# Moving one broadcast, some sums and one root in the middle of a two-layer mixer kernel

## The chip, the cores and the metric

The kernel runs on one NeuronCore of one Trainium2 chip. The metric is device time in microseconds (us). Before the change the median of three runs is 1218.71 us (1217.93 to 1219.3). Names of engines: PE is TensorE, DVE is VectorE, ACT is ScalarE, POOL is GpSimd, SP is the engine whose queue issues the transfers.

## The reference

Two layers of the same two blocks act on `x` (2048 tokens by 1024 channels, bfloat16). The weights of both layers are the same.

```python
def _A_ref(x, wqkv, wo):            # 32 heads of 32; window of 8 keys, 2 tokens apart
    ...
    logits = jnp.where(mask[None, None, :, :], logits, -1e9)
    attn = _softmax(logits, axis=-1)
    o = jnp.einsum("bhsw,bhswd->bhsd", attn, vg)
    ...
def _B_ref(x, w1, b1, w2, b2):      # a mixer over the tokens, 2048 -> 3584 -> 2048
    h = _layernorm(x, axis=-1)
    u = jnp.einsum("bsd,sf->bdf", h, w1) + b1
    u = _gelu(u)
    y = jnp.einsum("bdf,fs->bds", u, w2) + b2
    ...
x = x + _A_ref(_layernorm(x, axis=-1), A_wqkv, A_wo)
x = x + _B_ref(_layernorm(x, axis=-1), B_w1, B_b1, B_w2, B_b2)
# and both once more
```

## The kernel before, in words

The tokens are dealt to two residue classes (`c` = 0, 1), for the window steps by two; each class has 8 tiles (`i` = 0 to 7) of 128 tokens. `hT` holds the normalised input, transposed, 16 such tiles side by side. A layer goes through these stages:

- V = h · Wv. In the first layer `start_up` makes it plainly; in the second `Sevens.run` (L446 to 486) makes it with seven block products in place of eight.
- attention, in 32 visits (the loop over `vis`): scores, exponentials, mask, values, and the q and k of the next head group (L500). `qk_chunk` copies parts of q into `qB`, some of them with DMAs on SP (L513).
- the output projection (L616), then `gemm1` (L871), the first product of the mixer.
- the second product of the mixer: `gemm2f` in the first layer, `gemm2s` in the second. `gemm2f` normalises its output as well, transposes it into `hT` for the second layer, and makes V's sums ready.

**The products by sevens** take a 2x2 blocking of both factors. Sums and differences of blocks (`S`, `T`, `U`, on DVE, POOL and ACT) are multiplied, and results run through the banks of PSUM: PE makes a product, ACT copies the bank to a second one, and PE adds the next product to that copy. So a copy on ACT stands between two products of PE. The factors are float16, scaled by a power of two that keeps the sums in range. The power comes from a bound of the weights: a maximum by partition, stored to DRAM, read back by a broadcast to all partitions (`share_wv`, L400; `share_w2`, L756), reduced by DVE, and cut to its power of two (`powers`, L732). For V the bound of Wv is known in `start_up` (`top_wv` writes `mv2`, L345); `power_wv` (L405) makes `csv` and `civ`, which `Sevens.scale` (L412) and V's last steps use.

**`gemm2f`** (L1177 on) goes through 8 groups `i` of 256 output columns. Groups 0 and 1 are made plainly: four outputs each, of 28 matmuls (`tokens`, L1316 to 1321). In this time ACT takes bounds of the w2 columns still to come (`bounds`, L797): SP fetches a piece into a free place (`refill`, eight places in `hT` at first), ACT runs over it (L792). `share(4)` and `share(6)` broadcast the bounds for groups 4, 5 and 6, 7. Groups 2 to 7 go by sevens (`product`, L1223 to 1227, 14 matmuls each); while PE works at group `i`, ACT and DVE make the scaled blocks and sums for `i + 1` (`scaled`, `mix`). Each output tile is closed by `corner_add` or `quarter`, then `aggregate` (store to `xb`, mean and variance), `root` (two small ACT instructions) and `normalise` (DVE, then a transposing DMA into `hT`). Group 7 has no successor; there the four tiles of Wv are scaled (`sv[0].scale`) and V's sums made: `t_sum(n, j)` differences of Wv's blocks, `s_sum(i, n)` sums of blocks of token tile `i`, four for each of 8 tiles. The first two token tiles get their sums inside `gemm2f`, the others in `Sevens.run` (`ahead`), a pair ahead.

**What sets the order.** Each engine works strictly in the order of its queue. `chain_(engine, f)` (L232) pins an instruction behind the last one so placed on that engine, `in_order` does it for PE, so the order of the source is the order of the queues. Tiles come from pools with a fixed number of buffers, in rotation; a new tile waits for the last readers of the buffer it takes. The pools that matter are `w` (9 buffers: weights, `T`, `U2`), `q` (2 buffers: `qB`, `qa`, `Sw`), `go` (14 buffers: `g`, `oT`, `qs`, `Sv`), `pc` (2 buffers: `pc`, `bc`, `bcw`, `bcv`) and `x2` (6 buffers).

The start of `gemm2f`, in the order of its queues:

```python
        load_w(1)
        chain_("SP", share_wv)
...
        corner_add(0, 0, 1)
        power_wv()
        in_order(tokens, 0, 1)
        bounds(A, 5)
        del room[:5]
        share(4)
        refill(4)
```

Of the kernel before, what the change touches and what calls it, by code (L numbers as in the profile page):

```python
# [13 lines left out]
FP16 = mybir.dt.float16  # L14
# [3 lines left out]
P = 128  # L18
# [10 lines left out]
def kernel(  # L29
# [15 lines left out]
    nc = tc.nc  # L45
# [31 lines left out]
    qp = pool("qp", 2)  # L77
# [154 lines left out]
    def chain_(eng, f, *args, **kw):  # L232
        with tc.issue_after(last[eng].ins) if eng in last else nullcontext():
            last[eng] = f(*args, **kw)
# [161 lines left out]
    def fill_wv(wv):  # L396
        for j in range(KD // 2):
            chain_("SP", lambda: nc.sync.dma_start(out=wv[j][:], in_=wq_v[:, 2 * j:2 * j + 2, 2 * D:3 * D]))

    def share_wv():  # L400
        bcw["v"] = pcp.tile([P, P, 2], FP32, name="bcv", tag="pc")
        nc.sync.dma_start(out=mxvd[:], in_=mv2[:])
        return nc.sync.dma_start(out=bcw["v"][:], in_=mxvd[:].partition_broadcast(P))

    def power_wv():  # L405
        chain_("DVE", powers, 0, 1, bcw.pop("v")[:].rearrange("p q c -> p (q c)"), csv, civ)

    class Sevens:
# [21 lines left out]
            return hT[:, 4 * c:4 * c + 4, cols(r, i)]  # L430

        def s_sum(self, i, n):
            if i not in self.S:
                self.S[i] = gop.tile([P, 4, 4, P], FP16, name="Sv", tag="go")
            q = [self.S[i][:, k] for k in range(4)]
            x, y, op = [(self.a(i, 1, 0), self.a(i, 1, 1), ALU.add), (q[0], self.a(i, 0, 0), ALU.subtract),
                        (self.a(i, 0, 0), self.a(i, 1, 0), ALU.subtract), (self.a(i, 0, 1), q[1], ALU.subtract)][n]
            chain_("DVE", tt, nc.vector, q[n], x, y, op)
# [326 lines left out]
    def power_w2(i0):  # L765
        def ts(out, in0, sc):
            return nc.vector.tensor_scalar(out=out, in0=in0, scalar1=sc, scalar2=None, op0=ALU.mult)
        i1 = i0 + 2
        chain_("DVE", powers, i0, i1, bcw.pop(i0)[:].rearrange("p q i -> p i q"), cs2, ci2)
        k = st("k2", [P, 2])  # L770
        chain_("DVE", ts, inv2[:, i0:i1], ci2[:, i0:i1], gi[:])
        chain_("DVE", ts, ncs2[:, i0:i1], cs2[:, i0:i1], -1.0)
        chain_("DVE", ts, k[:], cs2[:, i0:i1], gs[:])
        b0, b1 = b2_sb[:, i0:i1, 0], b2_sb[:, i0:i1, 1]
        chain_("DVE", tt, nc.vector, bia[:, i0:i1, 0], b0, k[:], ALU.mult)
        chain_("DVE", tt, nc.vector, bia[:, i0:i1, 1], b1, b0, ALU.subtract)
        chain_("DVE", tt, nc.vector, bia[:, i0:i1, 1], bia[:, i0:i1, 1], k[:], ALU.mult)
# [399 lines left out]
    def gemm2f(g, src, dst, seam):  # L1177
# [59 lines left out]
        def load_w(i, ns=range(4)):  # L1237
            w.setdefault(i, [])
            for n in ns:
                f0, f1 = n * 8, min(n * 8 + 8, FT)  # L1240
                w[i].append(wt_("w2", [P, f1 - f0, 256]))
                chain_("SP", nc.sync.dma_start, out=w[i][n][:], in_=w2_v[:, f0:f1, i * 256:(i + 1) * 256])
# [66 lines left out]
        room[:] = [hT[:, m:m + 4, (c * NI + i) * P:(c * NI + i + 2) * P] for i in (6, 4) for c in range(DIL) for m in (0, 4)]  # L1309
        refill(8)  # L1310
        load_w(1)
        chain_("SP", share_wv)
        chain_(A, ln_exp_table)
        grp = [(0, 1), (1, 1), (0, 0), (1, 0)]

# [9 lines left out]
        bounds(A, 4)  # L1325
        corner(0, 0, 1, bk[0][0])
        corner_add(0, 0, 1)
        power_wv()
        in_order(tokens, 0, 1)
        bounds(A, 5)  # L1330
        del room[:5]
# [61 lines left out]
        for i in range(2, NI):  # L1393
            j = i + 1
            more = j < NI
            pa, pd, pb, pc = (t_[:] for t_ in (two("a") + two("m") if i % 2 else two("s") + two("s")))
            A22, S1, S2, S4 = q[i][:, 0], q[i][:, 1], U2[i], U4[i]
            load_x(i)
            in_order(product, pa, stripes(i, 0, 0), B11)
            chain_(A, move, pb, pa, scale=cs2[:, i:i + 1], bias=bia[:, i, 0:1])  # L1400
            if i == 2:
                corner(1, 1, 0, bk[1][3])
                corner_add(1, 1, 0)
            else:
                quarter(i - 1, 1, 0, prev)
            aggregate(i - 1, 1)
            root(i - 1, 1)
            mix(S4, S4, S2, ALU.subtract)
            normalise(i - 1, 1)
            in_order(product, pd, weights(S1), T1)  # L1410
            if more:
                units_a(j)
            Z = x2("z", [P, 512], FP32)
            if i == 2:
                chain_(A, move, Z[:], pd)
                scaled(j, q[j][:, 0], 1, 1)
            else:
                if more:
                    scaled(j, q[j][:, 0], 1, 1)
                else:  # L1420
                    sv[0].scale(0)
                chain_(A, move, Z[:], pd)
                if more:
                    scaled(j, q[j][:, 1], 0, 1)
                else:
                    sv[0].scale(2)
            in_order(product, pb, weights(S2), [T2k(k) for k in range(K)], False)
            mix(S1, A22, S2, ALU.subtract)
            S3 = S1
            if i == 2:  # L1430
                t4(*range(8, K))
                power_w2(6)
            chain_(A, move, pc, pb, bias=bia[:, i, 1:2])
            if i == 2:
                scaled(j, q[j][:, 1], 0, 1)
            if more:
                units_b(j)
                scaled(j, U2[j], 0, 0, range(2))
                mix(q[j][:, 1], q[j][:, 1], q[j][:, 0], ALU.add)
            in_order(product, pa, stripes(i, 1, 0), B21, False)  # L1440
            if i + 2 < NI:
                load_w(i + 2)
            else:
                seam(i + 2 - NI)
            corner(i, 0, 0, pa)
            corner_add(i, 0, 0)
            if more:
                scaled(j, U2[j], 0, 0, range(2, 4))
            else:
                sv[0].scale(1)  # L1450
                sv[0].scale(3)
                sv[0].t_sum(3, 0)
                sv[0].t_sum(1, 0)
            in_order(product, pc, weights(S3), NT3, False)
            Y = x2("y", [P, 512], FP32)
            chain_(V, tt, nc.vector, Y[:], Z[:], pc, ALU.add)
            quarter(i, 1, 1, Y[:])
            if more:
                mix(U2[j], q[j][:, 1], U2[j], ALU.subtract)
            else:  # L1460
                sv[0].t_sum(3, 1)
                sv[0].t_sum(1, 1)
            in_order(product, pb, weights(S4), B22, False)
            chain_(V, tt, nc.vector, Z[:], Z[:], pb, ALU.add)
            quarter(i, 0, 1, Z[:])
            if more:
                units_c(j)
                scaled(j, U4[j], 1, 0)
            aggregate(i, 0)
            root(i, 0)  # L1470
            normalise(i, 0)
            if not more:
                for n in range(2):
                    for m in range(2):
                        sv[0].s_sum(m, n)
                for m in range(2):
                    sv[0].t_sum(2, m)
            in_order(product, pc, weights(A22), [T4k(k) for k in range(K)], False)
            prev = pc
        i = NI - 1  # L1480
        quarter(i, 1, 0, prev)
        aggregate(i, 1)
        root(i, 1)
        for n in range(2):
            for m in range(2):
                sv[0].s_sum(m, 2 + n)
        for m in range(2):
            sv[0].t_sum(4, m)
        normalise(i, 1)

    sv = [None]
    NU = NG * DIL
# [1 line left out]
    for li in range(2):  # L1494
# [4 lines left out]
        if first:  # L1499
            wv, wts = load_wv(), [None, None]  # L1500
            start_up(v, wv)
            chain_("SP", load_qk, 0, wts)
            res = lambda c, i: xin_v[c, i]
        else:
            def ahead(p, n):
                if p == 2 and n == 0:
                    chain_("DVE", zero_p)
                elif p == 4 and n == 0:
                    chain_("DVE", zero_q)
                elif n and p + 2 < NI:  # L1510
                    for m in range(4):
                        for k in range(2):
                            sv[0].s_sum(p + 2 + k, m)

            sv[0].run(v, ahead)
            res = lambda c, i: rows(xb, c, i)
# [6 lines left out]
            in_order(qk_chunk, 0, wts, part, n)  # L1523
        for vis in range(2 * NU):
            u, b = divmod(vis, 2)
            if b == 0 and u % (2 * DIL) == 1 and u + 3 < NU:
                nxt = [None, None]
                chain_("SP", load_qk, u // (2 * DIL) + 1, nxt)
# [77 lines left out]
        def seam(n):  # L1606
            if n:
                chain_("SP", load_qk, 0, wts)
                return
            wv[:] = load_wv()  # L1610
            fill_wv(wv)
            sv[0] = Sevens(wv)

        gemm2f(g, xa[li], xb, seam)
        qB = new_qB()


# [28 lines left out]
```

## Time and profile before

| | |
|---|---|
| median of three runs | 1218.71 us |
| the profiled execution | 1215.23 us |
| its span, first to last instruction | 1213.5 us |
| mean granted PE clock | 0.996 |
| busy: PE, DVE, ACT, POOL | 1197.1, 779.6, 692.6, 124.8 us |
| plain groups 0 and 1 of `gemm2f` (L1319) | 432.42 to 480.77 us |
| groups 2 to 7 by sevens (L1225) | 480.77 to 618.43 us |
| V by sevens (L442) | 618.43 to 671.89 us |

The profile is of one execution. The rows of a timeline give the start in us from the first instruction, the time, the engine, the line of the kernel and `out<-in` by tile names; in brackets stands how long the engine had been idle, and which event ended this. DMAs are seen where SP issues them (SPq) and by the waits that their landing ends. The granted clock is the share of its full rate that PE was given. Busy time of an engine that nobody waits for costs nothing; what counts is where PE stands still.

### The profile page before, as it was taken

To read this page: it belongs to the slowest core of one execution; us is meant where nothing else is said; L and a number is where in the kernel's file an instruction comes from. 1 tells how busy PE (TensorE), PEld (TensorE's weight loads), DVE (VectorE), ACT (ScalarE), POOL (GpSimd) and SP (SyncE) were. 2 spreads that over 40 slices of the span, in tenths; PEclk is the share of its full clock that TensorE was granted. 3 is DMA by queue.
4 is the path that set the end of the run, shared out by engine and by line. 5 is a ranking of instruction groups with operands and counts; after the bars stand their busy time and mean duration, and the time that the engine had idled before them with its cause. 6 is when DMAs were issued, how large, how long until landed. Compare 5 with 4: busy or idle time off the path is not lost.

```text
span 1213.5 us, 20522 instructions
## 1 busy us (share of the span) xinstructions
PE 1197.1 (99%) x7972; PEld 549.1 (45%) x7972; DVE 779.6 (64%) x1513; ACT 692.6 (57%) x1164; POOL 124.8 (10%) x121
## 2 busy tenths in 40 slices
PE   9999999999999999899989999999999999999998
PEld 4444444444444444344434444444444444444444
DVE  7558887888786634956565588888711312785664
ACT  5657776578777775565645577764543434432342
POOL 0000000280000050000000000002821212100000
PEclk9999999999999999899999999999999999999999
DMA  8822333696766768866520222334946554165521
GB/s 243 148 62 71 84 104 96 216 264 169 216 193 181 222 169 187 189 162 174 166 70 18 62 69 69 112 100 154 304 139 178 176 171 147 62 191 132 155 78 35
DMA packets 248562, 174.12 MB, mean 143 GB/s; under 512 B 48401, under 2 KB 224785, under 8 KB 245137
## 3 DMA queue, kind: packets, MB, share of 16 engines
q1 hardware_dynamic: 248464, 172.82, 51.3%
q8 instruction: 62, 1.02, 0.4%
q14 instruction: 36, 0.29, 0.1%
HBM read 130.30 MB, written 30.43 MB: 132 GB/s over the span
## 4 chain that ended last, share of the span: by engine, by line
PE 89%; DMA 5%; DVE 2%; SPq 1%; ACT 1%; issue 0%; DVEq 0%
PE m L500 18%; PE s L871 11%; PE m L616 9%; PE s L1075 7%; PE m L871 7%; PE a L871 6%; PE s L1225 5%; PE m L1075 4%; PE s L297 3%; PE a L1075 3%; PE s L697 2%; PE a L1225 2%; PE m L1225 2%; PE s L531 2%; PE s L442 2%; DMA mxd<-mx 2%
## 5 line engine op out<-in xcount | busy, mean ns | idle before, releaser
L500 PE MATMUL m<-hT,wqk 128*128 128x512 bf16 x1024 | 231.8, 380 | 0.0
L547 DVE TENSOR_TENSOR Pm<-pc,band 32x640 bf16<-32x640 bf16 x256 | 123.6, 483 | 45.1 <-ACT pc L535 38.3
L500 PEld LDWEIGHTS <-wqk 128*128 128x128 bf16 x1024 | 95.3, 98 | 117.9 <-issue 10.7
L871 PEld LDWEIGHTS <-Sw 128*128 128x128 f16 x832 | 81.4, 98 | 99.2 <-issue 1.2
L616 PE MATMUL m<-wo,oT 128*128 128x512 bf16 x512 | 111.8, 379 | 0.0
L871 PEld LDWEIGHTS <-w 128*128 128x128 f16 (+1 forms) x624 | 61.1, 98 | 73.6
L711 POOL TENSOR_TENSOR T<-h 128x512 f16<-128x512 bf16 x16 | 18.4, 1153 | 621.9 <-DMA xr<-xb 372.9
L616 PEld LDWEIGHTS <-oT 128*128 128x128 bf16 x512 | 49.6, 98 | 60.6 <-issue 1.8
L711 DVE TENSOR_TENSOR py<-pz,m 128x512 f32<-128x512 f32 x14 | 9.6, 687 | 90.4 <-PE m L871 62.1
L535 ACT ACTIVATE pc<-s,shift 128x320 bf16<-128x320 f32 x128 | 60.8, 530 | 11.2 <-PE s L531 11.2
L871 PE MATMUL s<-T,Sw 128*128 128x512 f16 x288 | 66.2, 379 | 0.9 <-ACT s L880 0.9
L507 ACT CAST qs<-m 128x512 bf16<-128x512 f32 x64 | 37.5, 585 | 44.4 <-PE m L500 42.0
L504 ACT CAST kT<-m 128x512 bf16<-128x512 f32 x64 | 37.5, 585 | 41.9 <-PE m L500 38.8
L711 POOL TENSOR_TENSOR Pm<-g 128x512 f16<-128x512 bf16 x24 | 27.7, 1168 | 283.0 <-ACT Pm L792 164.2
L623 DVE TENSOR_TENSOR xn<-m,xr 128x512 bf16<-128x512 f32 x64 | 44.1, 689 | 15.2 <-PE m L616 15.0
L871 PE MATMUL a<-h,w 128*128 128x512 bf16 x224 | 52.9, 379 | 0.0
L871 PE MATMUL m<-T,Sw 128*128 128x512 f16 x224 | 52.9, 379 | 0.0
L656 ACT ACTIVATE h<-xn,bi,rs 128x1024 bf16<-128x1024 bf16 x32 | 39.7, 1240 | 23.1 <-DVE bi L642 23.1
L847 ACT ACTIVATE w<-w,cs 128x2048 f16<-128x2048 bf16 x26 | 51.8, 1997 | 0.0
L1075 PEld LDWEIGHTS <-u 128*128 128x128 f16 x336 | 32.8, 98 | 39.7
L711 DVE TENSOR_TENSOR xs<-tq,xs 128x512 bf16<-128x512 f32 (+1 forms) x30 | 21.2, 710 | 45.1 <-ACT tq L1230 27.9
L511 DVE COPY qB<-qs 32x512 bf16<-32x512 bf16 x136 | 38.2, 281 | 18.5 <-ACT qs L507 15.6
(251 smaller groups left out, 2189.0 us busy)
## 6 DMA issues: line engine op xcount, KB each, us to landing
w<-in_B_w_dram SPq DMA_DIRECT2D x110, 512.0 KB, 6.0
sd<-Sw SPq DMA_DIRECT2D x13, 1024.0 KB, 8.3
Sw<-sd SPq DMA_DIRECT2D x13, 1024.0 KB, 4.9
wqk<-in_A_wqkv_dram SPq DMA_DIRECT2D x16, 512.0 KB, 4.9
xa<-xn SPq DMA_DIRECT2D x32, 256.0 KB, 2.8
xs<-xa SPq DMA_DIRECT2D x32, 256.0 KB, 3.2
Pm<-in_B_w_dram SPq DMA_DIRECT2D x26, 256.0 KB, 6.4
wo<-in_A_wo_dram SPq DMA_DIRECT2D x8, 512.0 KB, 5.4
```

Of the source, the lines that this page charges most:

```text
L500: mm = nc.tensor.matmul(ps[:], lhsT=wts[part][:, kt, (g % 2) * P:(g % 2 + 1) * P], rhs=hT[:, kt, lo:lo + 512], start=(kt == 0), stop=(kt = ...
L511: nc.vector.tensor_copy(out=qB[u % 2][hp, h, ls], in_=qs[hp, :])
L535: nc.scalar.activation(out=pc[:, 2 * n:2 * n + 2].rearrange("p t h k -> p (t h k)"), in_=ss[n][:, 0:2 * HG * GW], func=ACT.Exp, scale=scal ...
L547: mm = nc.vector.tensor_tensor(out=Pm[rp, :, s0:s0 + HB, r * KG:r * KG + GW].rearrange("p h t k -> p t h k"), in0=pc[rp], in1=mk, op=ALU.mult)
L616: mm = nc.tensor.matmul(ps[:], lhsT=oT[g][:, cols(c, i)], rhs=wo[n][g // 4][:, g % 4, :], start=(g == 0), stop=(g == NG - 1))
L623: return nc.vector.tensor_tensor(out=xn[:, xs_], in0=pss_["o", n][:], in1=xr[:, xs_], op=ALU.add)
L656: last["ACT"] = nc.scalar.activation(out=h2[c][i][:], in_=xn[:], func=ACT.Identity, bias=t["bi"][:], scale=t["rs"][:])
L711: return eng.tensor_tensor(out=out, in0=a, in1=b, op=op)
L847: return nc.scalar.activation(out=w[:].bitcast(FP16), in_=w[:], func=ACT.Identity, scale=cs[:, fb + 1:fb + 2])
L871: r = nc.tensor.matmul(out, lhsT=lhs[:, k, :], rhs=rhs[k], start=start and k == 0, stop=stop and k == NI - 1, skip_group_check=True)
L1075: r = nc.tensor.matmul(out, lhsT=lhs[k], rhs=rhs[k][:, cols_], start=start and k == 0, stop=k == K - 1, skip_group_check=True)
L1225: r = nc.tensor.matmul(out, lhsT=lhs[k], rhs=rhs[k], start=start and k == 0, stop=k == K - 1, skip_group_check=True)
```

## The change

1. `share_wv` is split. The store of the bound to DRAM (`keep_wv`) is issued by SP in visit 5 of the first layer's attention. The broadcast back is issued by SP in group 3 of `gemm2f`, after `load_w(5)`, no longer at the start of `gemm2f`.
2. `power_wv` moves on DVE from the start of `gemm2f` to group 5.
3. In group 7 all eight sums of the first two token tiles, and the differences `T3`, `T1`, `T2`, are made earlier on DVE. These sums get one tile of their own in the `q` pool; before they were two tiles of the `go` pool. `scale(1)` and `scale(3)` move on ACT ahead of a bank copy of group 7.
4. The last `root` and `normalise` leave `gemm2f`: they come back as the function `rest`, which `Sevens.run` calls after its first four ACT instructions (two bank copies and two Z).

```diff
+    def keep_wv():
+        return nc.sync.dma_start(out=mxvd[:], in_=mv2[:])
+
     def share_wv():
         bcw["v"] = pcp.tile([P, P, 2], FP32, name="bcv", tag="pc")
-        nc.sync.dma_start(out=mxvd[:], in_=mv2[:])
         return nc.sync.dma_start(out=bcw["v"][:], in_=mxvd[:].partition_broadcast(P))
...
         def s_sum(self, i, n):
+            if i == 0 and n == 0:
+                both = qp.tile([P, 2, 4, 4, P], FP16, name="Sv", tag="q")
+                self.S[0], self.S[1] = both[:, 0], both[:, 1]
...
         load_w(1)
-        chain_("SP", share_wv)
         chain_(A, ln_exp_table)
...
         corner_add(0, 0, 1)
-        power_wv()
         in_order(tokens, 0, 1)
...
                 power_w2(6)
+            if i == 5:
+                power_wv()
+            if not more:
+                sv[0].scale(1)
+                sv[0].scale(3)
+                for n in range(4):
+                    for m in range(2):
+                        sv[0].s_sum(m, n)
             chain_(A, move, pc, pb, bias=bia[:, i, 1:2])
...
                 load_w(i + 2)
+                if i == 3:
+                    chain_("SP", share_wv)
             else:
                 seam(i + 2 - NI)
+            if not more:
+                for m in range(2):
+                    sv[0].t_sum(3, m)
+                    sv[0].t_sum(1, m)
             corner(i, 0, 0, pa)
             corner_add(i, 0, 0)
             if more:
                 scaled(j, U2[j], 0, 0, range(2, 4))
-            else:
-                sv[0].scale(1)
-                sv[0].scale(3)
-                sv[0].t_sum(3, 0)
-                sv[0].t_sum(1, 0)
...
             else:
-                sv[0].t_sum(3, 1)
-                sv[0].t_sum(1, 1)
+                for m in range(2):
+                    sv[0].t_sum(2, m)
...
-            if not more:
-                for n in range(2):
-                    for m in range(2):
-                        sv[0].s_sum(m, n)
-                for m in range(2):
-                    sv[0].t_sum(2, m)
...
         aggregate(i, 1)
-        root(i, 1)
-        for n in range(2):
-            for m in range(2):
-                sv[0].s_sum(m, 2 + n)
         for m in range(2):
             sv[0].t_sum(4, m)
-        normalise(i, 1)
+
+        def rest():
+            root(i, 1)
+            normalise(i, 1)
+
+        return rest
...
             def ahead(p, n):
-                if p == 2 and n == 0:
+                if p == 0 and n == 0:
+                    rest()
+                elif p == 2 and n == 0:
...
+            if first and vis == 5:
+                chain_("SP", keep_wv)
...
-        gemm2f(g, xa[li], xb, seam)
+        rest = gemm2f(g, xa[li], xb, seam)
```

## The prediction

> **What bounds the kernel now.** I read the page first: TensorE (PE) is busy 1197.1 us of a span of 1213.5, and 89% of the chain that ended last is PE. So only time in which PE stands, or runs at a lower clock, can be won. The waits of PE give that time by line.
>
> ```profile
> PE s L1225 <- ACT s L1230: 5.8, 1, 5.8
> PE m L442 <- ACT m L453: 3.0, 1, 3.0
> PE s L1225 <- DVE g L711: 1.2, 1, 1.2
> ```
>
> The reader is to see that two single waits, in `gemm2f` (L1225) and at the start of V by sevens (L442), and one small one make 10 us; the change touches exactly these stages. Next the table of busy time by stretch around both waits (columns: stretch, its length, PE, PEld, DVE, ACT, POOL busy with counts, granted clock, DMA share, GB/s).
>
> ```profile
> 497.00:499.00 2.00, 2.00 (x6) 0.69 (x5) 1.93 (x5) 0.83 (x3) 0.00 (x0) 0.50 1.19 265
> ...
> 627.00:629.00 2.00, 2.00 (x6) 0.71 (x5) 0.17 (x1) 0.93 (x2) 0.00 (x0) 0.50 0.31 63
> ```
>
> After both waits the granted clock is 0.50: matmuls start 0.43 us apart instead of 0.216. After PE's 0.90 us wait for ACT at 411.7 it is 1.00 (the row of 410 to 415). A long wait therefore costs more than itself. Then the chain of waits from 440 us on (start, us, what):
>
> ```profile
> 444.40 5.19 DMA mxvd<-mv
> 449.65 3.74 DMA bcv<-mxvd
> ...
> 454.51 0.16 DVE mx L758
> 454.69 2.91 DMA mxw<-mx
> ...
> 458.02 5.62 DMA hT<-in_B_w_dram
> ```
>
> and the timeline (start, us, engine, line; in brackets the idle time before, and who ended it):
>
> ```profile
> 453.41 0.42 DVE L735 TENSOR_REDUCE m<-bcv 128x1 f32<-128x256 f32 x1 [11.93 <-DMA bcv<-mxvd]
> ...
> 493.48 0.29 ACT L1275 ACTIVATE ln<-mv,eps 128x1 f32<-128x1 f32 x1 [5.17 <-DVE mv L1271]
> ...
> 495.70 5.04 PE L1225 MATMUL s<-T,u 128*128 128x512 f16 x14 [5.79 <-ACT s L1230]
> ...
> 624.25 0.29 ACT L1275 ACTIVATE ln<-mv,eps 128x1 f32<-128x1 f32 x1 [4.79 <-DVE mv L1271]
> ```
>
> The 5.79 us wait begins 50 us earlier: `power_wv` makes DVE wait 11.93 us for the broadcast `bcv`. Behind it in DVE's order stands the reduction of `share(4)`; SP waits for that before it issues the next eight fetches of w2 (`hT<-in_B_w_dram`); ACT's bounds wait 12.14 us for those (463.67), and the load of group 2's w2 stands behind them on SP. DMA moves 10 GB/s in 448 to 450 and nothing in 456 to 458. From 483.55 DVE works without a gap and is late; ACT's copy of the bank (494.93 to 495.66) stands behind the root of 493.48, which waits 5.17 us for DVE. The last line is the same pattern at V's start: a root that waits for DVE, with ACT's bank copies queued behind it.
>
> **1. The broadcast out of the start of `gemm2f`.** What PE loses there: from the first product of group 2 (480.77) to the start of its fourth (500.58) are 19.81 us. Three products at the 3.02 us from start to start of groups 3 to 7 are 9.07. Lost: 10.74, of which 1.9 is half clock.
>
> What is next late: without `mxvd`, SP is free at 444.36 and the reduction runs as soon as ACT's five bounds are done (444.84), so `mxw` is issued near 445.0 instead of 454.69. Its landing is the unknown: 2.9 (this store at 454.69, DMA idle) to 8.8 us (median of `mxd<-mx`, DMA full). I take 449.6, where `mxvd`, issued 444.40 behind the same loads of w2, landed. The fetches then start at 450.0 instead of 458.02: 8.0 us earlier. I move the rest of the chain by that, after checking that nothing in it waits for PE, which does not move: token products end at 450.5, 456.6, 468.7, 474.7 and 480.77, and their new users stand at 451, 460, 472, 478 and 488. Group 2's w2 lands by 471 instead of 479; DVE's series ends at 485.4; the bank copy ends at 487.7 (495.66 less 8.0). PE wants it at 480.77 + 6.05 = 486.8. So 0.9 us of wait is left. The next copy stands on ACT behind a root, Z and four scalings and ends at 494.0, where PE is ready at 493.7: 0.2 more. Lost after: 1.1. **Gain 9.6.**
>
> **2. V's start.** From 618.43 (first product) to 671.89 (first matmul of L500) are 53.46 us; 56 products at 0.863 (46 of them from 632.18 on) are 48.3. Lost: 5.1, that is the 2.98 wait, 1.7 of half clock and small waits for `Sv` and `T`. After, ACT copies each bank when its product ends (0.58 each), Z follows, and the root of the last tile stands behind these; its mv comes about 2.5 us after V's start and its root runs about 4.3 us after it, so neither waits. `Sv` and three `T` are made before. The last `normalise` comes late, but its transposed columns are read only by the sums for tiles 6 and 7, near 659. **Gain 5.1.**
>
> A rule to weigh: the Trainium skill, page "TensorE: Matmul & The Clock Gate", section "Part 1: The HAM clock gate", has the clock halve only after a whole idle window of about 3.4 us. By that the 2.98 us wait would have cost no clock, this gain would be 3.4, the sum 11.9 and the time 1206.9; the trace's 0.50 in 627 to 629 speaks against it, so it gets no chance of its own.
>
> **3. What group 7 pays.** ACT's order there was scale(0), Z, scale(2), bank copy; now scale(1) and scale(3) stand ahead of the copy too.
>
> ```profile
> 604.01 1.99 ACT L414 ACTIVATE wv<-wv,csv 128x2048 f16<-128x2048 bf16 x1
> ...
> 606.54 0.66 ACT L1230 ACTIVATE m<-m,bia 128x512 f32<-128x512 f32 x1 [0.54 <-PE m L1225]
> ...
> 609.36 2.75 PE L1225 MATMUL m<-Pm,qa 128*128 128x512 f16 x12
> ```
>
> Three scalings at 1.94 from start to start from 604.01 end at 609.8, the copy at 610.5; PE wants that bank at 609.36. **Loss 1.15**, all on PE. Its effect on the clock lies between nothing (0.90 us wait, clock 1.00) and 1.7 (2.98 us wait); 1.15 is nearer the first: nothing.
>
> **4. Costs under cover.** `power_wv` in group 5: five small DVE instructions, 453.41 to 454.6, 1.2 us, ahead of a 1.59 us DVE wait for ACT (563.36); were that cover gone, the next group's sum would be 1.2 late, and PE needs it 10 us later. Eight `Sv` sums at 0.34 (2.7 us) run from 604.1, where DVE would wait anyway: `T3` takes a w2 tile that PE frees near 609. The four differences then end at 611.75 instead of 610.37 for the corner's sum; the next DVE step that PE feeds is at 613.5. SP: `mxvd` now goes out in visit 5, between qB copies that end near 93 and begin again at 99.5; `bcv` after the loads that end at 527.1, with SP idle until 532.65. The sums in the `q` pool take the buffer of group 6's qa, last read at 597.3, before 604. All zero; up to 0.3 if a qB copy were late (the one such wait of PE is 0.3).
>
> **Sum.** -9.6 - 5.1 + 1.15 = -13.5. The profiled execution took 1215.23 (its span 1213.5), so 1201.7; the median of the runs, 1218.71, lies 3.5 above it, and less the same 13.5 that is **1205.2**.
>
> **The rivals.** *The store lands late*: 8.8 us, as `mxd<-mx`. The fetches start at 454.2, only 3.8 earlier; the wait is 5.0 and the clock halves (1.7): gain 4.0 in place of 9.6, time 1210.8. For it: DMA is full to 448; against: `mxvd` took 5.19 there. *It lands early*, 2.9: fetches at 448.3, the wait goes altogether, 10.6: 1204.2, and 1203 without the wait of part 3. *V still waits*: the first copies stand behind the root of tile (7, 0), whose mv comes near 619.3; PE needs the copies at 623, so 2.9 us of delay on DVE brings the old wait back: 1210.3. *It does not do what it says*: the wait in group 2 has another source (fetches or loads bound by DMA traffic): only parts 2 and 3 are left, -4.0, 1214.7. Against it: DMA is idle for 12 us while the chain waits. *Slower*: group 7's ACT queue. If a wv piece lands late, both scalings and the copy behind them wait and PE with them; the loss is landing + 2.65 - 609.36, which outweighs 14.7 of gain only from a landing at 621.4 on. Issued by 588.9 with at most 8.3 us to landing, they are there at 597; the price that is sure is 1.15.
>
> **How the numbers follow.** Chances: forecast 0.60, early 0.12, late 0.13, V still waits 0.06, does not do it 0.05, slower 0.04. The range 1200.5 to 1211 holds the first four (0.91), with 3 us below for runs as quick as the profiled one, less something for what I did not see. About 0.2% (2.4 us) is what a measurement of this kernel can tell from no change. Faster: the first four and most of the fifth, 0.92; same 0.04; slower 0.04.
>
> **What would show it.** Right: no DVE wait for `bcv`; `mxw` issued near 445 and fetches from 450; a PE wait of about 1 us or less at the first `T,u` product of group 2 with clock 1.00; a new wait of 1.1 us for ACT in group 7; V's 56 products in 48.5 us. Wrong: `mxw` landing after 452, a clock of 0.50 anywhere after 480, or a wait at L442's successor.

## The result and the profile after

The changed kernel took 1201.9 us (median of 4 runs, 1200.14 to 1204.17) beside 1218.32 us for the kernel before (4 runs): ratio **0.9871**, 95% interval 0.9846 to 0.9896. The prediction was 1205.2, a ratio of 0.9889 to the median that it started from. The profiled execution fell from 1215.23 to 1200.14 us, its span from 1213.5 to 1198.4: 15.1 less, where 13.5 were forecast.

First the chain that ended last, on the page of the kernel after (shares of the span):

```profile
PE 97%; DMA 1%; ACT 1%; DVE 0%; issue 0%; DVEq 0%
```

It was 89% PE before. What remains of PE's waits (in all, times, longest, us):

```profile
PE s L318 <- DVE warm L111: 1.1, 1, 1.1
PE m L1230 <- ACT m L1235: 0.9, 1, 0.9
PE s L536 <- ACT kT L509: 0.7, 1, 0.7
```

The waits of 5.8 and 3.0 us are gone, and so is the 1.2 us wait for DVE; at 0.9 stands a new one, that of group 7. (The changed file is longer: L1225 of before is L1230, L442 is L447, L453 is L458, L1230 is L1235, L1275 is L1280.) The timeline of SP shows the chain of the bounds:

```profile
443.35 0.81 SPq L765 DMA_DIRECT2D mxw<-mx  x1
449.39 0.34 SPq L766 DMA_DIRECT2D bcw<-mxw  x1
449.82 4.38 SPq L793 DMA_DIRECT2D hT<-in_B_w_dram  x5
```

The fetches start at 449.82 (458.02 before, forecast 450.0). Then, on ACT and on PE, what they lead to:

```profile
484.99 0.73 ACT L1235 ACTIVATE s<-s,bia,cs 128x512 f32<-128x512 f32 x1
```

```profile
486.18 3.19 PE L1230 MATMUL s<-T,u 128*128 128x512 f16 x14
```

No bracket with an idle time stands behind the `T,u` product of 486.18, so PE did not wait for the bank copy, which ended at 485.72, with 0.46 us to spare. Group 7 and V's start, ACT and PE:

```profile
592.64 5.78 ACT L416 ACTIVATE wv<-wv,csv 128x2048 f16<-128x2048 bf16 x3
598.32 0.65 ACT L1235 ACTIVATE m<-m,bia 128x512 f32<-128x512 f32 x1
...
609.14 0.57 ACT L458 COPY m<-a 128x512 f32<-128x512 f32 x1 [0.59 <-PE a L447]
...
612.31 0.28 ACT L1280 ACTIVATE ln<-mv,eps 128x1 f32<-128x1 f32 x1
```

```profile
599.01 2.75 PE L1230 MATMUL m<-Pm,qa 128*128 128x512 f16 x12 [0.86 <-ACT m L1235]
...
611.53 1.03 PE L447 MATMUL m<-T,Sv 128*128 128x512 f16 x4
```

Three scalings stand ahead of the bank copy, and PE waits 0.86 us for it. At V's start the copy (609.14) goes first and the root (612.31) runs behind it. The stretches of group 2's three products and of V (length; PE, PEld, DVE, ACT, POOL busy; granted clock, DMA share, GB/s) hold no lost time and full clock:

```profile
480.14:489.21 9.07, 9.07 (x44) 4.12 (x43) 8.90 (x21) 3.82 (x10) 0.00 (x0) 1.00 1.14 273
608.07:656.42 48.35, 48.35 (x225) 21.91 (x224) 30.20 (x50) 25.65 (x43) 0.00 (x0) 1.00 0.12 32
```

So the 15.1 us come from: group 2, 19.81 to 9.07, 10.7; V, 53.46 to 48.35, 5.1; small waits ahead of group 2, 0.6 (PE reaches it at 480.14 instead of 480.77); less 1.0 in group 7 (594.96 + 3.02 = 597.98 wanted, 599.01 got); and 0.3 more lost in the rest, mostly in one wait of PE at the scores of layer 2 (L531 before, L536 after), which lies between 0.3 and 1.4 in the profiles of this study. The 0.6 are no gain of the change: the ten profiled executions of this study reach group 2 anywhere from 480.14 to 480.91, whichever kernel it is.

### The profile page after: what moved, and what is told of

It is laid out like the page before. It is cut to its first block, busy times and chain, and to the rows that moved or that the text cites. A ratio compares the mean times of both kernels' runs of the same rounds, so it can differ in the third digit from the quotient of the medians.

```text
span 1198.4 us, 20518 instructions
## 1 busy us (share of the span) xinstructions
PE 1191.6 (99%) x7972; PEld 548.5 (46%) x7972; DVE 780.6 (65%) x1513; ACT 692.9 (58%) x1164; POOL 125.6 (10%) x121
## 4 chain that ended last, share of the span: by engine, by line
PE 97%; DMA 1%; ACT 1%; DVE 0%; issue 0%; DVEq 0%
PE m L505 19%; PE s L876 11%; PE m L621 9%; PE m L876 7%; PE s L1080 7%; PE a L876 6%; PE s L1230 5%; PE m L1080 4%; PE s L297 3%; PE a L1080 3%; PE m L1230 3%; PE s L702 2%; PE s L536 2%; PE s L447 2%; PE s L1323 2%; PE a L1230 2%
## 5 line engine op out<-in xcount | busy, mean ns | idle before, releaser
L505 PEld LDWEIGHTS <-wqk 128*128 128x128 bf16 x1024 | 95.3, 98 | 117.9 <-issue 10.7
L516 DVE COPY qB<-qs 32x512 bf16<-32x512 bf16 x136 | 38.2, 281 | 18.5 <-ACT qs L512 15.5
```

The costliest lines, as they stand in the source:

```text
L505: mm = nc.tensor.matmul(ps[:], lhsT=wts[part][:, kt, (g % 2) * P:(g % 2 + 1) * P], rhs=hT[:, kt, lo:lo + 512], start=(kt == 0), stop=(kt = ...
L516: nc.vector.tensor_copy(out=qB[u % 2][hp, h, ls], in_=qs[hp, :])
```

## The experiments

Theory at the start: two stalls, independent of each other. Group 2's is a chain through DVE's and SP's order that begins at the broadcast; V's is a bank copy behind a root. Rivals: one cause for both; the store's round trip alone; V's gain from the early sums; group 7's wait from elsewhere than the scalings. The first four kernels ran on one chip beside 9 runs of the kernel before (median 1215.97).

**The broadcast alone.** The kernel before, with the store in visit 5, the broadcast in group 3 and the power in group 5; V's end as before.

```diff
+    def keep_wv():
+        return nc.sync.dma_start(out=mxvd[:], in_=mv2[:])
...
-        nc.sync.dma_start(out=mxvd[:], in_=mv2[:])
...
         load_w(1)
-        chain_("SP", share_wv)
...
         corner_add(0, 0, 1)
-        power_wv()
...
+            if i == 5:
+                power_wv()
...
+                if i == 3:
+                    chain_("SP", share_wv)
...
+            if first and vis == 5:
+                chain_("SP", keep_wv)
```

> The kernel before with only the broadcast moved: store in visit 5, broadcast in group 3, power in group 5; group 7 and V's start as before. Theory 'two stalls, independent': the wait of 5.8 us in group 2 and its half clock go, 10.7 us less than before (about 1207.5 where before is 1218.3); V's start still waits 3 us for a bank copy and loses 5 us. Rival 'one cause': the late DVE at the start of gemm2f also makes V's start late; then V's wait goes too and this kernel is within 1 us of the changed one (16 less than before).

1204.16 us, ratio 0.9901 (0.9887 to 0.9914): 11.8 less. Group 2 has no wait. PE's largest wait is the old one at V's start:

```profile
PE m L444 <- ACT m L455: 3.0, 1, 3.0
```

The first stall goes alone and the second stays. In the profiled execution the clock stayed at 1.00 behind this wait, and V lost 3.4 us instead of 5.1 (607.69 to 659.48, less 48.35). That may account for the 1.1 us beyond the expected 10.7; the last section says why the clock differs.

**V's end alone.** The changed kernel with the broadcast and the power back at the start of `gemm2f` (the edit above, reversed).

> The changed kernel with the broadcast and its power put back to the start of gemm2f: only the early sums, the two scalings ahead of the bank copy and the last root behind the copies are left. Theory 'two stalls, independent': 5.1 us less at V's start, 1.0 us more in group 7, 4.1 less than before; the 5.8 us wait in group 2 stays. Rival 'one cause': V's start waits as before and only the 1.0 us of group 7 is seen, so slower than before by about 1.

1211.23 us, ratio 0.996 (0.9947 to 0.9974): 4.7 less (4.1 expected). V takes 48.34 us without a wait; group 2's stays:

```profile
PE s L1228 <- ACT s L1233: 5.8, 1, 5.8
```

The parts add up to within 1 us: 11.8 + 4.7 = 16.5, and both together gave 15.5 (the changed kernel run again, below, against its own kernel before). "One cause" falls.

**The fourth scaling behind the bank copy.**

```diff
                 sv[0].scale(1)
-                sv[0].scale(3)
...
             chain_(A, move, pc, pb, bias=bia[:, i, 1:2])
+            if not more:
+                sv[0].scale(3)
```

> The changed kernel with one scaling of Wv, scale(3), put behind the bank copy of group 7 on ACT; scale(1) stays ahead. Theory: the copy ends at about 597.1 on the time scale of the changed kernel's profile, PE wants it at 598.0, so the wait of 0.9 goes and the kernel is 1.0 us faster than the changed one; the differences on DVE come 0.5 later and nobody on PE notices. Rival: something else on ACT or DVE is late right behind (the corner's copy, T3's second half) and takes the same 1 us; then no change.

1200.4 us, ratio 0.987 (0.9857 to 0.9884). ACT's timeline of this kernel:

```profile
592.91 3.88 ACT L416 ACTIVATE wv<-wv,csv 128x2048 f16<-128x2048 bf16 x2
596.70 0.65 ACT L1235 ACTIVATE m<-m,bia 128x512 f32<-128x512 f32 x1
597.27 2.00 ACT L416 ACTIVATE wv<-wv,csv 128x2048 f16<-128x2048 bf16 x1
```

The copy has one scaling less ahead of it, and PE goes from one product to the next without a wait (595.24 to 598.26). The changed kernel itself did not run in this series, so the median has nothing to stand against here; both ran together later, below.

**The root alone, without early sums.** The first kernel of this section, and in addition the last root and its normalise behind the first copies of V; sums, scalings and differences where they were.

```diff
-        root(i, 1)
...
-        normalise(i, 1)
+        def rest():
+            root(i, 1)
+            normalise(i, 1)
...
+                if p == 0 and n == 0:
+                    rest()
...
```

> The changed kernel without the early sums: Wv's scalings, differences and the first token tiles' sums stand where they stood before, in two tiles of the go pool; the broadcast is moved and the last root and normalise stand behind the first bank copies and Z. Theory: V's start waits for the root alone; without the early sums PE waits 0.3 for the first Sv and 0.6 to 1 for T2, and group 7 does not pay its 1.0, so the time is the changed kernel's within 1 us. Rival: the sums on DVE are what V's start waits for; then about 3 us of wait with half clock stay there and the kernel is 4 us slower than the changed one.

1200.08 us, ratio 0.9866 (0.9853 to 0.988): as fast as the whole change (0.9873 in the next series), within the intervals. PE's timeline at V's start:

```profile
608.15 1.03 PE L444 MATMUL s<-wv,hT 128*128 128x512 f16 x4
609.29 1.04 PE L444 MATMUL a<-wv,Sv 128*128 128x512 f16 x4
...
611.03 1.06 PE L444 MATMUL m<-T,Sv 128*128 128x512 f16 x4
```

The first product with `Sv` starts 1.14 us after the one ahead of it instead of 0.86, since `Sv` came 0.28 late; the one with `T`, where the root's wait stood, follows two products later without a gap. With the root out of the way, that is all that the early sums bring; and group 7 has no wait here. Moving the root is enough to end V's stall, and the price in group 7 was paid for 0.3 us. Whether the early sums alone would have ended it too, by letting DVE reach the root's input sooner, no run tells.

The next four ran on one chip (kernel before 1216.03, 6 runs).

**The changed kernel again, and the fourth scaling late again.**

> The changed kernel once more, so that it stands on one chip with the next three. Both theories: 15.7 less than before (ratio 0.987).

> The changed kernel with scale(3) behind the bank copy, once more beside the changed one. Theory: 1.0 us faster than the changed kernel of the same call. Rival (the same 1 us is taken by something else): no difference.

1200.5 us (1200.28 to 1201.08; ratio 0.9873, 0.9855 to 0.989) and 1199.92 (1199.02 to 1200.12; ratio 0.9866, 0.985 to 0.9881). No run of the second is as long as any of the first, so the wait in group 7 does come from the scaling; its 1.0 us show as 0.6 in the medians. The second has the lowest median of the study, though the root alone (1200.08) can't be told from it.

**Store and broadcast at the old place, the power late.** DVE then waits for nothing, but SP's queue holds both transfers ahead of the chain.

```diff
-    def keep_wv():
-        return nc.sync.dma_start(out=mxvd[:], in_=mv2[:])
...
     def share_wv():
...
+        nc.sync.dma_start(out=mxvd[:], in_=mv2[:])
...
         load_w(1)
+        chain_("SP", share_wv)
...
-                if i == 3:
-                    chain_("SP", share_wv)
...
-            if first and vis == 5:
-                chain_("SP", keep_wv)
```

> The changed kernel with store and broadcast of V's bound back at the start of gemm2f on SP; power_wv stays in group 5, so DVE waits for nothing there. Theory 'two queues hold the chain': SP holds the broadcast until the store has landed (near 449.4), so the next store goes out near 449.8 and not 443.4, the eight fetches start near 453.1 and not 449.8, and the copy in group 2 comes 2.8 us after PE wants it: 2.8 us slower than the changed kernel, 4.5 if the clock halves. Rival 'only the wait on DVE counts': as fast as the changed kernel.

1209.48 us, ratio 0.9949 (0.9933 to 0.9965): 9.0 slower than the changed kernel. SP's timeline:

```profile
444.29 1.53 SPq L402 DMA_DIRECT2D mxvd<-mv  x1
449.41 0.34 SPq L403 DMA_DIRECT2D bcv<-mxvd  x1
449.85 0.38 SPq L763 DMA_DIRECT2D mxw<-mx  x1
...
455.59 5.56 SPq L791 DMA_DIRECT2D hT<-in_B_w_dram  x5
```

DVE's reduction ran at 442.94, yet `mxw` goes out at 449.85, behind the broadcast that waits for its store; and `mxw`, issued right behind the broadcast, takes 5.3 us to land. The rival (only DVE's wait counts; as fast as the changed kernel) falls: SP's queue holds the chain too. PE lost 9.4 us at group 2 (480.91 to 499.40, less 9.07), more than the theory's 2.8 or 4.5: 5.8 of wait, 2.3 of half clock in the third product, and 1.3 at the second, whose matmuls follow DVE's sums, 0.34 us apart. `mxw` took 2.4 us longer than the 2.9 that the theory had, and the loads behind it were slower as well (below). V's end alone, which has DVE's wait besides, lost 10.6 us there (480.34 to 499.98, less 9.07): taking the wait off DVE alone won 1.2 of them.

**Only the store early.** The changed kernel with broadcast and power at their old places.

```diff
         load_w(1)
+        chain_("SP", share_wv)
...
         corner_add(0, 0, 1)
+        power_wv()
...
-            if i == 5:
-                power_wv()
...
-                if i == 3:
-                    chain_("SP", share_wv)
```

> The changed kernel with only the store of V's bound early (visit 5); the broadcast is issued at its old place on SP and power_wv stands at its old place on DVE. Theory: the broadcast lands near 449.4 behind the loads of w2, power_wv and the reduction behind it end near 450.7, the store of the next bound lands near 453.7, the fetches start near 454, 4.2 later than in the changed kernel; PE waits 3.8 us in group 2: 3.8 slower than the changed kernel, 5.5 if the clock halves. Rival 'the store's round trip was the cost': within 1 us of the changed kernel.

1207.78 us, ratio 0.9929 (0.9912 to 0.9947): 7.3 slower than the changed kernel. DVE's timeline:

```profile
449.23 0.42 DVE L740 TENSOR_REDUCE m<-bcv 128x1 f32<-128x256 f32 x1 [8.20 <-DMA bcv<-mxvd]
```

Without its store ahead of it the broadcast still makes DVE wait 8.20 us; the fetches start at 453.89 (454 expected) and PE waits 5.40 us at group 2. The rival (the store's round trip was the cost) falls as the whole cause. It is a part: PE lost 7.1 us at group 2 (480.31 to 496.46, less 9.07), 3.5 less than in V's end alone, where the store too stands at its old place. The forecasts had 3.8 or 5.5; though the fetches started on time, the last piece of w2 came late. ACT's timeline, as it takes the last two pieces:

```profile
473.02 0.72 ACT L1209 ACTIVATE qa<-w,cs 128x512 f16<-128x512 bf16 x1 [1.15 <-DMA w<-in_B_w_dram]
475.27 0.51 ACT L1209 ACTIVATE qa<-w,cs 128x256 f16<-128x256 bf16 x1 [1.53 <-DMA w<-in_B_w_dram]
```

In the kernel before, ACT waited 0.15 us for the same last piece (479.07), not 1.53. The next section comes back to this.

## Why the prediction was right, and where a size was off

**1. The broadcast: gain 10.7, forecast 9.6.** The chain was read rightly. `mxw` went out at 443.35 and landed at 449.38 (forecast 445.0 and 449.6), the fetches began at 449.82 (450.0), 8.2 earlier. It went out earlier than forecast because the reduction ran at 442.17 and not at 444.84 (it does not wait for the last of the bounds that the forecast counted); SP, busy until 443.25 with loads, then set the moment. That the landing hardly moved with it bears out the forecast's choice of a moment, the one at which `mxvd` had landed behind the same loads, and not of a duration. The step that failed is "I move the rest of the chain by that", and with it "0.9 us of wait is left" and "0.2 more": group 2's last w2 piece landed at 469.1 instead of 479.05, 9.95 earlier, and the bank copy ended 9.94 earlier, so nothing was left. The transfers themselves were quicker. From the first fetch to that landing:

| kernel | first fetch | to the last w2 landing, us |
|---|---|---|
| after; again; scaling late again | 449.8; 449.9; 450.6 | 19.3; 19.7; 19.6 |
| broadcast alone; scaling late; root alone | 450.1; 449.5; 450.0 | 19.7; 19.8; 19.4 |
| before; V's end alone | 458.0; 457.7 | 21.0; 21.1 |
| store early; share at old place | 453.9; 455.6 | 21.4; 21.8 |

Six kernels whose chain starts early need 19.3 to 19.8, four whose chain starts late 21.0 to 21.8. The first fetch lands 5.3 to 5.9 us after issue in the six and 5.6 to 6.5 in the four, so most of the difference comes later. The DMA records of the traces show where. The eight fetches and the four loads of group 2's w2 are 7680 packets of 512 bytes; 98% of them are through 18.3 to 18.9 us after the first fetch in the six kernels and 18.7 to 19.5 in the four. In the six the last packet ends 0.3 to 0.5 us after that; in the four 32 to 46 packets trail, and the last ends 1.7 to 1.8 us after. In all ten executions one packet of 16 KB, of the queue that the profile calls instruction, moves near 470.7 to 472.6 and takes 0.9 to 1.2 us. In the four it falls among these loads, in the six 2.7 us or more behind the last of them. The kernel with the store early shows it piece by piece: the packet moves from 472.24 to 473.42. The pieces that ACT takes before its end (471.15 and 473.02) come 6.6 and 8.5 us after the first load's issue, and 6.6 and 8.4 in the changed kernel; the last one comes 10.7 us after it, and 9.3 there. So about 1.7 of the 9.95 us are loads that end before this packet moves, which the forecast did not know of: that the wait went altogether is luck in this part. That the packet holds up the loads fits all ten executions; the records don't name the DMA engine that moved a packet, and no run moved it by itself, so the cause is not shown.

**2. V's start: 5.1, as forecast, by the step given.** The copies went ahead, the root ran 4.2 us after V's start (forecast 4.3), and PE waits for neither. The forecast gave no separate share to the early sums; the runs do: 0.3 us (the root alone).

**3. Group 7: loss 1.03, forecast 1.15**, from the scalings (the late fourth scaling), and the clock stayed at 1.00.

**4. Under cover: nothing, as forecast.** `power_wv` in group 5 (550.3) and the bound's broadcast (issued 515.9, landed 4.8 us later) make nobody wait.

**The weighed rule.** The forecast set the half clock of 627 to 629 against "whole idle window". That was too simple, as the next section shows: the clock changes by windows on a fixed grid, and the broadcast alone had a wait of 2.99 us at the same place without the half clock. By that, 1.7 of V's gain hangs on where the wait falls in the grid, and the forecast had it from one execution. The runs of the kernel before that stand beside the experiments show mean clocks of 0.994 to 0.996, and the profiled one 0.996, so about as much half clock is usual there.

**The rivals.** "The store lands early" came nearest in its result (the wait at group 2 gone altogether, 10.6) though not in its reason: the store landed 6.0 us after issue, not 2.9, and the loads behind it were quicker. "Late", "V still waits" and "does not do what it says" show nowhere. "Slower" is there at its sure price alone.

**The sum.** 15.1 instead of 13.5 in the profiled execution. The median lay 3.3 below the forecast. The other 1.7 are the scatter of the runs: the forecast laid 3.5 us between the profiled execution and the median, as in the kernel before, and in the changed kernel they lie 1.8 apart. The base was high as well: the first three runs of the kernel before (1218.71) lie above its median in both later series (1215.97 and 1216.03). The forecast ratio, 0.9889, lies inside the measured interval.

## What to carry to other kernels

Follow a stall back through every in-order queue that its data passes, the one that issues DMAs too: here a small broadcast of no urgency stood ahead of eight urgent fetches on SP and, through its consumer, on DVE, and taking the wait off DVE alone won 1.2 of 10.6 us. When a split and a reorder come in one change, run them apart: the root behind the copies won nearly all that both won together, and the sums' price in group 7, 1.0 us in the traces, could be saved. When a chain is moved, its transfers need not keep their durations; a margin under 1 us says neither "wait" nor "no wait".

## What the runs showed of the hardware that was not expected

**The clock halves by windows on a fixed grid.** The changes of the granted clock lie whole multiples of 3.413 us apart through each execution; in the kernel before, 143, 2, 37, 1 and 171 such windows lie between them. Cut along that grid (columns as above), the kernel before:

```profile
489.26:492.67 3.41, 0.65 (x2) 0.13 (x2) 3.34 (x7) 0.00 (x0) 0.00 (x0) 1.00 1.01 203
492.67:496.08 3.41, 0.38 (x1) 0.10 (x1) 3.38 (x10) 2.57 (x6) 0.00 (x0) 0.50 1.20 293
622.38:625.79 3.41, 0.47 (x3) 0.23 (x3) 3.34 (x9) 1.51 (x5) 0.00 (x0) 1.00 0.35 88
625.79:629.20 3.41, 3.41 (x10) 1.18 (x9) 1.38 (x3) 2.21 (x4) 0.00 (x0) 0.50 0.25 49
```

The broadcast alone, whose 2.99 us wait falls across the border of two windows, and V's end alone:

```profile
609.46:612.87 3.41, 2.02 (x9) 0.80 (x9) 3.38 (x8) 0.00 (x0) 0.00 (x0) 1.00 0.86 78
612.87:616.28 3.41, 1.69 (x8) 0.78 (x8) 3.38 (x9) 2.73 (x7) 0.00 (x0) 1.00 0.26 80
616.28:619.70 3.42, 3.42 (x17) 1.57 (x16) 0.69 (x2) 2.27 (x4) 0.00 (x0) 1.00 0.40 77
```

```profile
488.35:491.76 3.41, 1.25 (x4) 0.29 (x3) 3.38 (x8) 0.00 (x0) 0.00 (x0) 1.00 0.88 152
491.76:495.17 3.41, 0.00 (x0) 0.00 (x0) 3.34 (x10) 1.96 (x5) 0.00 (x0) 0.50 1.21 300
```

The window after one with PE busy 0.47, 0.65 or 1.25 us has clock 0.50; after 2.02 and 1.69 us it keeps 1.00. So the same wait at V's start costs about 3.0 us or 4.7, by its phase in the grid. It varies between runs of one kernel too: of the broadcast alone, two runs show a mean clock of 1.0 (1203.4 and 1203.9 us) and two 0.999 (1204.4 and 1205.1), which fits, though only one of them has a trace. The limit lies between 1.25 and 1.69 us of busy time as far as these rows go. The Trainium skill, page "TensorE: Matmul & The Clock Gate", section "Part 1: The HAM clock gate", has a free-running window of 4096 cycles, 3413 ns; the grid agrees with it, but an "idle" window here may hold 1.25 us of matmuls.

**A store's way to landing depends on what is queued.** The same `mxw<-mx` landed 2.9 us after issue with DMA idle (before), 5.3 right behind the broadcast (share at the old place) and 6.0 behind the loads of w2 (after). The transfer is the same 1 KB each time, so its size alone does not give its round trip.
